# Four large PSUM tiles in place of three large and two small ones, from the seventh token group of the up phase on

## The chip, the cores and the metric

The kernel runs on one core of a Trainium2 chip. The metric is the time on the device in microseconds (us); a kernel's time is the median of its runs.

## The reference

```python
x = _attn_ref(q, k, v, tau)            # 2304 tokens x 512
x = _moe_ref(x, modality_id, ...)      # one of 8 experts per token
logits = x @ w_gate
P = np.exp(logits - logits.max())
for _ in range(8):
    P /= P.sum(1, keepdims=True) + 1e-09
    P /= P.sum(0, keepdims=True) + 1e-09
    P *= N / E
for e in range(E):                     # 8 experts, all of them for every token
    h = np.maximum(x @ w1[e], 0.0)     # 512 -> 1024
    out += P[:, e:e + 1] * (h @ w2[e]) # 1024 -> 512
```

The change touches the last loop, the dense mixture, in which every token goes through all 8 experts.

## The kernel before, in words

The program has three stretches: attention, the routed mixture, and the dense mixture. The dense mixture has an *up phase* (`x @ w1`, `up()`, L1142) and a *down phase* (`h @ w2`, the loop at L1422). Both use Strassen's scheme: a matrix product in 2 x 2 blocks is made of seven block products, numbered 0 to 6, whose sums give the four output blocks. float32 is kept by splitting each operand into a rounded part and a rest, and by adding three products of these; the two parts are made by `both()` (L939): ScalarE casts (L937), VectorE subtracts (L941).

Up phase: 8 experts, two column halves of each, three token groups: `n_up` = 48 groups, counted by `n` (L1329). In each group `product()` (L1129) issues 12 matmuls of 128 x 384 for each of the seven block products, in the order `ORD` = 0, 2, 1, 4, 3, 6, 5 (L90). After each product VectorE and ScalarE read the finished PSUM tile (L1172 to L1200), and `hook(b)` then issues pieces of other work.

Three large PSUM tiles A, B, C of two banks each take the products. In a group they have three roles: `ch` takes products 0, 1, 3 and 5, one added to the other; `cc` takes product 2; `cb` takes product 4 and then, from a fresh start, product 6. The roles move on by one tile from group to group (L1144).

Who reads them, on ScalarE's and VectorE's queues:

- after 0, 1 and 3, ScalarE copies `ch` to x (L1173, L1175, L1181);
- after 1, VectorE adds `cc` into h12; after 3, it adds `cc` into h22 and weighs h22 (L944, L1137);
- after 4, VectorE adds `cb` into h11 and weighs h11;
- after 6, VectorE adds `cb` into h12, weighs it, and forms two differences on VectorE and one on GpSimd;
- after 5, VectorE weighs `ch` into h21 and forms one more difference.

"Weigh" is `weigh()` (L1136): the larger of the value and 0, times the token's weight. All seven results are stored to DRAM (`save()`, L1152).

The weights of the next column half are made in every third group (`u == 2`, L1347): `make_up()` (L964) puts one cast on ScalarE and one subtraction on VectorE (L941, `w1c<-wr` or `w1c<-x`) behind each product, and GpSimd makes two of their sums.

Two small PSUM tiles of one bank each (`small()`, L987) serve the gate in the first six groups, by the generators `steps` and `later`. They stay open to the end of the up phase. Then they are closed, and a fourth large tile D takes their place (L1366, L1367). The down phase uses all four: each token group holds one tile over four experts, and `buf()` (L1370) hands them out in turn.

The order on each engine's queue is that in which the program calls the instructions (`manual_schedule`, L1478).

Of the kernel before, what the change touches and what calls it, by code (L numbers as in the profile page):

```python
# [7 lines left out]
F32 = mybir.dt.float32  # L8
# [7 lines left out]
PSUM = bass.MemoryType.PSUM  # L16
DRAM = bass.MemoryType.DRAM

B, H, S, D = 4, 8, 576, 64
# [69 lines left out]
UN = 384  # L89
# [8 lines left out]
def _program(ctx, tc, qT, kT, vv, tau, wg, mod, mbias, cst, wA, wg2, wU, wD, out):  # L98
    nc = tc.nc
    P = 128  # L100
# [8 lines left out]
    pd = dram.tile([2, 72, P], F32, name="pd")  # L109
# [665 lines left out]
    def experts(es):  # L775
# [167 lines left out]
        def op2(eng, out, x, y, op):  # L943
            eng.tensor_tensor(out=out, in0=x, in1=y, op=op)  # L944

        def cut(t, lo, k, n):
            return t[:, lo:lo + k * n].rearrange("p (k n) -> p k n", k=k)
# [35 lines left out]
        ps_m = es.enter_context(tc.tile_pool(name="pm", bufs=1, space=PSUM, reuse_waits="tile"))  # L983
        pt_s = ExitStack()
        ps_t = pt_s.enter_context(tc.tile_pool(name="pt2", bufs=2, space=PSUM, reuse_waits="tile"))
        bank = lambda tag: ps_m.tile([P, 2, 512], F32, tag=tag, name="q" + tag)
        small = lambda: ps_t.tile([P, 512], F32, tag="t", name="t")  # L987

        X = [[[cut(t, (2 * b + i) * 2 * UN, 2, UN) for i in range(2)] for b in range(7)] for t in (xb, xa, xc)]
# [134 lines left out]
        def load_p(dst, e, u):  # L1124
            for t in range(2):
                nc.sync.dma_start(
                    out=dst[t], in_=pd[t].rearrange("(e u t) n -> e u (t n)", e=E, u=NU)[e, u].partition_broadcast(P))

        def product(q, first, a, b, nk):  # L1129
            for j, (l, r) in enumerate(((0, 0), (1, 0), (0, 1))):  # L1130
                for i in range(2):
                    for k in range(nk):
                        mm(q[:, i, 0:UN], lhsT=a[l][:, k, 128 * i:128 * i + 128], rhs=b[r][:, k],  # L1133
                           start=first and k == 0 and j == 0, stop=k == nk - 1 and j == 2, skip_group_check=True)

        def weigh(out, src, pv, n=2):  # L1136
            V.scalar_tensor_tensor(out=out, in0=src, scalar=0.0, in1=bc(pv.unsqueeze(1), [P, n, UN]), op0=ALU.max, op1=ALU.mult)  # L1137

        def relu(out, src):
            A.activation(out=out, in_=src, func=AF.Relu)  # L1140

        def up(n, e, g, u, hook):  # L1142
            order = (0, 4, 2, 1, 6, 3, 5) if n < 3 else ORD
            ch, cb, cc = (bank("ABC"[(i - n) % 3])[:, :, 0:UN] for i in range(3))  # L1144
            where = {0: ch, 1: ch, 3: ch, 5: ch, 2: cc, 4: cb, 6: cb}
            h11, h12, h22, h21 = quad[n if n < 3 else n % 2]
            if n == 0:
                h11 = cut(pbx, 720, 2, UN)
            t1, t2, t3, t4 = quad[2]
            pv = pbs[n % 2]  # L1150

            def save(b, src):  # L1152
                nc.sync.dma_start(out=hd[e, u, b, :, 2 * g:2 * g + 2], in_=src)

            todo = []

            def fin(x, src, t, b):
                if e:
                    weigh(x, src, pv[t])
                    save(b, x)  # L1160
                elif src is x:
                    todo.append((x, b))
                else:
                    relu(x, src)
                    save(b, x)

            plus = lambda out, x, y: op2(V, out, x, y, ALU.add)
            minus = lambda eng, out, x, y: op2(eng, out, x, y, ALU.subtract)
            for b in order:
                product(where[b], b in (0, 2, 4, 6), wu[b], X[u][b], 2)  # L1170
                ready, todo[:] = list(todo), []
                if b == 0:  # L1172
                    A.copy(out=h11, in_=ch)  # L1173
                elif b == 1:
                    A.copy(out=h12, in_=ch)  # L1175
                    plus(h12, cc, h12)
                elif b == 4:
                    plus(h11, cb, h11)
                    fin(h11, h11, 0, 0)
                elif b == 3:  # L1180
                    A.copy(out=h22, in_=ch)  # L1181
                    plus(h22, cc, h22)
                    fin(h22, h22, 1, 6)
                elif b == 6:
                    plus(h12, cb, h12)
                    if e:
                        weigh(h12, h12, pv[1])
                        minus(V, t1, h12, h11)
                        save(2, t1)
                        minus(G, t3, h22, h12)  # L1190
                        minus(V, t2, h22, t1)
                        save(1, t2)
                        save(3, t3)
                    else:
                        fin(h12, h12, 1, 2)
                elif b == 5:
                    fin(h21, ch, 0, 4)
                    if e:
                        minus(V, t4, h21, t2)
                        save(5, t4)  # L1200
                for x, s in ready:
                    relu(x, x)
                    save(s, x)
                hook(b)
# [8 lines left out]
        def chained(*its):  # L1213
            for it in its:
                yield from it
# [21 lines left out]
        xs, steps, later = chained(xs, make_x(1), make_x(2)), gates(), sink()  # L1237
        D = {}
# [90 lines left out]
        for n in range(n_up):  # L1329
            k, u = divmod(n, NU)  # L1330
            e, g = divmod(k, 2)

            def hook(b):
                at = (ORD if n >= 3 else (0, 4, 2, 1, 6, 3, 5)).index(b)
                for _ in range(2):
                    next(xs, None)
                if next(steps, False) is False and (n > 2 or n == 2 and at > 2):
                    next(later, None)
                if 2 * NU - 1 <= n < n_up - 1 and at == (1 if n >= 2 * NU else 5):
                    e2, u2 = divmod(n + 1, 2 * NU)  # L1340
                    load_p(pbs[(n + 1) % 2], e2, u2 % NU)
                if k < 2 * E - 1:
                    if (u, at) == ((0, 0) if k else (1, 2)):
                        ld_up(k + 1)
                    elif u == 1 and at in (4, 6):
                        sums_up(k + 1, at // 2 - 2)
                    elif u == 2:  # L1347
                        make_up(k + 1, b)
                elif u == 1:
                    if at == 0:  # L1350
                        w_load(0, 0, 0)
                        h_load(0)
                        for j in range(1, 4):
                            w_load(0, j, 0)
                    elif at == 6:
                        w_make(0)
                elif u == 2:
                    if at in (0, 3, 6):
                        h_make(at // 3)

            up(n, e, g, u, hook)
            if n == n_up - NU:
                open_down()

        open_rest()
        pt_s.close()  # L1366
        ps_d = es.enter_context(tc.tile_pool(name="pd", bufs=1, space=PSUM, reuse_waits="tile"))  # L1367
        turns = [0]

        def buf(tag=None):  # L1370
            if tag is None:
                tag = "ABCD"[turns[0] % 4]
                turns[0] += 1
            return (ps_d if tag == "D" else ps_m).tile([P, 2, 512], F32, tag=tag, name="r" + tag)

        done, half, sent = [0], [None], []

        def put(*tiles):
            q = buf("CCCCDCADC"[done[0]])
            done[0] += 1  # L1380
            at = [9 * t + 3 * u + j for u, t, j in tiles]
            for h, i in enumerate(at):
                for d in range(4):
                    nc.tensor.transpose(q[:, h, 128 * d:128 * d + 128], x2[:, d, 128 * i:128 * i + 128], ident)
            o = D["o"][done[0] % 4]
            A.copy(out=o, in_=q)
            for h, i in enumerate(at):
                G.memset(idx_0, 0)
                ins = G.indirect_dma_start(out=out, in_=o[:, h], in_offset=None,
                                           out_offset=bass.IndirectOffsetOnAxis(ap=idx_c[:, i:i + 1], axis=0))  # L1390
                for x in sent:
                    tc.declare_no_dep(ins.ins if hasattr(ins, "ins") else ins, x, reason="rows of a permutation")
                sent.append(ins.ins if hasattr(ins, "ins") else ins)
# [27 lines left out]
        q = [None] * NU  # L1421
        for n, (m, u) in enumerate(SEQ):  # L1422
            i, b, e = STEPS[m]
# [54 lines left out]
    with tc.manual_schedule():  # L1478
        with ExitStack() as es:
            attention(es)  # L1480
        with ExitStack() as es:
            experts(es)
# [88 lines left out]
```

## Time and profile before

| | us |
|---|---|
| runs of the kernel | 2083.52, 2086.37, 2086.32 |
| median | 2086.32 |
| the profiled execution, its own time | 2085.2 |
| its span, first to last instruction | 2083.4 |
| TensorE busy in it (PE) | 2000.8 |
| VectorE busy (DVE) | 1560.4 |
| ScalarE busy (ACT) | 870.8 |
| GpSimd busy (POOL) | 484.6 |

All times in the trace are counted from the start of the span. The up phase runs from about 583.6 to 1320.8 us, the down phase from there to the end. The trace gives start and duration of each instruction, and for idle time what ended it. A matmul's row is its own time of 0.33 us; in a row of matmuls they overlap, so a product of 12 matmuls has a duration of 2.24 us while the next product starts 2.08 us after it. Starts, not durations, tell how fast TensorE advances. Names are the program's: qA is large tile A in the up phase, rA the same in the down phase.

### The profile page before, as it was taken

The numbers are of one execution on the slowest core, as the hardware profiler recorded it, in microseconds if no ns is written. First come the engines' busy times: TensorE is split into PE (matmuls) and PEld (weight loads), VectorE is DVE, ScalarE is ACT, GpSimd is POOL, SyncE is SP. The second block draws the span as 40 slices with busy tenths as digits, with TensorE's granted clock in tenths as the row PEclk, the third lists the DMA queues.
The fourth block names the chain that finished last, engine by engine and source line by source line (L and its number), as shares of the span: only waits on it lengthen the run. The fifth ranks groups of instructions, "written<-read, shape, count | busy, mean of one in ns | idle before, by whom it ended". The sixth has DMA issues, their size and how long they took to land.

```text
span 2083.4 us, 32556 instructions
## 1 busy us (share of the span) xinstructions
PE 2000.8 (96%) x12677; PEld 1906.7 (92%) x12677; DVE 1560.4 (75%) x1957; ACT 870.8 (42%) x1152; POOL 484.6 (23%) x395
## 2 busy tenths in 40 slices
PE   8999998999989999999999999999999999899997
PEld 7777777999979999999999999999999999899997
DVE  7788886666576799888989898856766568777672
ACT  6777763555554322222222222444443443343433
POOL 5564625052021233232333232000000000000004
PEclk9999998999999999999999999999999999999999
DMA  5232324666523566766676776965565776776753
GB/s 191 74 120 98 98 64 155 203 204 207 187 84 107 195 224 226 244 239 233 226 238 219 240 244 219 405 243 182 185 213 203 247 270 244 254 264 242 252 209 131
DMA packets 177215, 421.12 MB, mean 202 GB/s; under 512 B 16397, under 2 KB 126365, under 8 KB 177053
## 3 DMA queue, kind: packets, MB, share of 16 engines
q1 hardware_dynamic: 170700, 399.03, 56.1%
q0 software_dynamic: 4928, 19.93, 2.5%
q8 instruction: 102, 1.67, 0.3%
q14 instruction: 61, 0.49, 0.1%
q10 hardware_dynamic: 1424, 0.01, 0.0%
HBM read 274.91 MB, written 143.99 MB: 201 GB/s over the span
## 4 chain that ended last, share of the span: by engine, by line
PE 38%; DVE 13%; issue 12%; DMA 5%; ACT 2%; POOL 0%; SPq 0%; POOLq 0%; ACTq 0%; DVEq 0%
PE rB L1431 6%; PE rA L1431 6%; PE rD L1431 6%; PE qB L1133 5%; PE rC L1431 5%; PE qC L1133 5%; PE qA L1133 5%; DVE x L944 5%; DVE x L1137 3%; DMA pbx<-pd 3%; DVE w1c L941 2%; DVE df L944 1%; DVE xa L941 1%; ACT xa L937 1%; DMA hd<-x 1%
## 5 line engine op out<-in xcount | busy, mean ns | idle before, releaser
L944 POOL TENSOR_TENSOR x<-x 128x768 f32<-128x768 f32 x45 | 114.9, 2554 | 462.2 <-DVE x L1137 368.3
L941 DVE TENSOR_TENSOR w1c<-df,w1c 128x1536 fp32r<-128x1536 f32 x84 | 146.4, 1756 | 88.5 <-ACT w1c L937 88.4
L941 DVE TENSOR_TENSOR xa<-df,xa 128x1536 fp32r<-128x1536 f32 (+1 forms) x100 | 166.6, 1670 | 59.7 <-ACT xa L937 59.5
L937 ACT CAST xa<-df 128x1536 fp32r<-128x1536 f32 (+1 forms) x100 | 140.4, 1412 | 157.5 <-DVE df L944 69.3
L944 DVE TENSOR_TENSOR x<-x 128x768 f32<-128x768 f32 x135 | 196.3, 1454 | 4.9 <-DVE xb L944 0.5
L937 ACT CAST w1c<-df 128x1536 fp32r<-128x1536 f32 x84 | 123.5, 1481 | 147.0 <-DVE df L944 55.9
L1324 POOL DMA_DIRECT2D hd<-df x12 | 6.6, 550 | 612.4 <-DVE df L944 612.4
L1133 PE MATMUL qB<-xc,w1c 128*128 128x384 f32 x768 | 143.7, 335 | 2.9 <-DVE x L944 1.9
L1133 PE MATMUL qC<-xa,w1c 128*128 128x384 f32 x768 | 144.0, 335 | 1.5 <-ACT x L1181 1.5
L1133 PE MATMUL qA<-xb,w1c 128*128 128x384 f32 x768 | 144.0, 335 | 0.2 <-ACT x L1181 0.2
L478 DVE TENSOR_REDUCE cols<-s 128x1 f32<-128x576 f32 x144 | 105.0, 755 | 51.7 <-PE s L473 51.0
L1133 PEld LDWEIGHTS qB<-xc,w1c 128*128 128x128 f32 x768 | 133.9, 188 | 3.5 <-issue 2.2
L1133 PEld LDWEIGHTS qA<-xb,w1c 128*128 128x128 f32 x768 | 134.0, 188 | 2.7 <-issue 2.1
L1133 PEld LDWEIGHTS qC<-xa,w1c 128*128 128x128 f32 x768 | 133.7, 188 | 1.8 <-ACT x L1181 1.8
L489 ACT ACTIVATE sa<-s,cols 128x576 f32<-128x576 f32 x144 | 103.4, 741 | 65.2 <-DVE cols L478 65.2
L1137 DVE SCALAR_TENSOR_TENSOR x<-x,pbx 128x768 f32<-128x768 f32 x126 | 125.8, 999 | 4.3
L172 DVE TENSOR_TENSOR colr<-cols,colr 128x1024 fp32r<-128x1024 f32 x57 | 72.8, 1281 | 56.4 <-ACT colr L171 56.2
L473 PE MATMUL s<-colr 128*128 128x288 f32 x640 | 110.0, 310 | 4.6 <-DVE cols L500 1.2
L1431 PE MATMUL rA<-xa 128*128 128x384 f32 x576 | 105.9, 339 | 5.7 <-ACT xa L937 5.7
L1431 PEld LDWEIGHTS rA<-xa 128*128 128x128 f32 x576 | 101.4, 190 | 6.6 <-ACT xa L937 6.6
L473 PEld LDWEIGHTS s<-colr 128*128 128x128 f32 x640 | 89.1, 189 | 18.8 <-issue 14.3
L1431 PE MATMUL rB<-w1c,xa 128*128 128x384 f32 x552 | 99.8, 335 | 0.0
(292 smaller groups left out, 4451.7 us busy)
## 6 DMA issues: line engine op xcount, KB each, us to landing
df<-hd SPq DMA_DIRECT2D x180, 768.0 KB, 4.9
hd<-x SPq DMA_DIRECT2D x317, 384.0 KB, 3.1
cols<-wA SPq DMA_DIRECT2D x84, 512.0 KB, 4.6
pbx<-pd SPq DMA_DIRECT2D x114, 192.0 KB, 5.1
wr<-wU SPq DMA_DIRECT2D x16, 768.0 KB, 6.2
dg<-wD SPq DMA_DIRECT2D x20, 512.0 KB, 8.0
hd<-df POOLq DMA_DIRECT2D x12, 768.0 KB, 7.3
cols<-qT SPq DMA_DIRECT2D x15, 576.0 KB, 4.1
```

What stands on the lines that cost most here:

```text
L172: sub.tensor_tensor(out=lo[i], in0=raw, in1=hi[i].bitcast(F32), op=ALU.subtract)
L473: mm(s[:, hf, 0:288], lhsT=l, rhs=r, start=n == 0, stop=n == len(ops) - 1)
L478: V.tensor_reduce(out=mx[:, i % 18:i % 18 + 1], in_=St[i][:, :, 0:288], axis=AX.XY, op=ALU.max, negate=True)
L489: A.activation(out=e.rearrange("p (h c) -> p h c", h=2), in_=St[i][:, :, 0:288], func=AF.Exp, bias=mxs[i // 18 % 2][0][:, i % 18:i % 18 + 1])
L937: A.copy(out=out, in_=in_)
L941: sub.tensor_tensor(out=hi_lo[1], in0=src, in1=hi_lo[0].bitcast(F32), op=ALU.subtract)
L944: eng.tensor_tensor(out=out, in0=x, in1=y, op=op)
L1133: mm(q[:, i, 0:UN], lhsT=a[l][:, k, 128 * i:128 * i + 128], rhs=b[r][:, k], start=first and k == 0 and j == 0, stop=k == nk - 1 and j == 2 ...
L1137: V.scalar_tensor_tensor(out=out, in0=src, scalar=0.0, in1=bc(pv.unsqueeze(1), [P, n, UN]), op0=ALU.max, op1=ALU.mult)
L1324: G.dma_start(out=hd[0, u, b], in_=x)
L1431: mm(q[u][:, i2, 0:UN], lhsT=a[l][:, k, 128 * i2:128 * i2 + 128], rhs=h[r][:, k], start=first and k == 0 and j == 0, stop=last and k == 3 ...
```

## The change

From group `n` = 6 on (`NOLD`), the two small tiles are closed and tile D is open in their place. The gate's generator is run to its end first; after the sixth group it has nothing left to issue. Each group then has four roles: `ch` for products 0, 1, 3 and 5, `cb` for product 4, `cd` for product 6, and `cc` for product 2. `cc` is D in every group; A, B and C rotate: a group's `ch` is the group before's `cb`, its `cb` that group's `cd`, and its `cd` that group's `ch`. The down phase hands out the same four tiles, beginning with the last group's `cb`, then `cc`, `cd` and `ch`, and its output steps take the same turns under the new names.

```diff
+        NOLD, role, ps_4 = 6, [], []
+        bank = lambda tag: (ps_4[0] if tag == "D" else ps_m).tile([P, 2, 512], F32, tag=tag, name="q" + tag)
...
         def up(n, e, g, u, hook):
-            ch, cb, cc = (bank("ABC"[(i - n) % 3])[:, :, 0:UN] for i in range(3))
-            where = {0: ch, 1: ch, 3: ch, 5: ch, 2: cc, 4: cb, 6: cb}
+            if n < NOLD:
+                ch, cb, cc = (bank("ABC"[(i - n) % 3])[:, :, 0:UN] for i in range(3))
+                cd = cb
+            else:
+                if n == NOLD:
+                    role[:] = ["ABC"[(2 - n + 1) % 3], "ABC"[(1 - n + 1) % 3], "D", "ABC"[(1 - n) % 3]]
+                else:
+                    role[:] = [role[1], role[3], role[2], role[0]]
+                ch, cb, cc, cd = (bank(r)[:, :, 0:UN] for r in role)
+            where = {0: ch, 1: ch, 3: ch, 5: ch, 2: cc, 4: cb, 6: cd}
...
-                    plus(h12, cb, h12)
+                    plus(h12, cd, h12)
...
+            if n == NOLD:
+                for _ in later:
+                    pass
+                pt_s.close()
+                ps_4.append(es.enter_context(tc.tile_pool(name="pd", bufs=1, space=PSUM, reuse_waits="tile")))
             up(n, e, g, u, hook)
...
-        pt_s.close()
-        ps_d = es.enter_context(tc.tile_pool(name="pd", bufs=1, space=PSUM, reuse_waits="tile"))
+        spare = "".join(role[i] for i in (1, 2, 3, 0))
...
-                tag = "ABCD"[turns[0] % 4]
+                tag = spare[turns[0] % 4]
...
-            q = buf("CCCCDCADC"[done[0]])
+            q = buf(spare[(2, 2, 2, 2, 3, 2, 0, 3, 2)[done[0]]])
```

The number and order of the instructions stay the same on every engine; the tiles that they name change, and with these the waits. TensorE's queue, before, in one group in which weights are made (n = 26, operand `xc`, seven products in the order 0, 2, 1, 4, 3, 6, 5) and the first four products of the next (n = 27, operand `xb`):

```order
L1133 MATMUL qB<-xc,w1c 128x384 x12
L1133 MATMUL qA<-xc,w1c 128x384 x12
L1133 MATMUL qB<-xc,w1c 128x384 x12
L1133 MATMUL qC<-xc,w1c 128x384 x12
L1133 MATMUL qB<-xc,w1c 128x384 x12
L1133 MATMUL qC<-xc,w1c 128x384 x12
L1133 MATMUL qB<-xc,w1c 128x384 x12
L1133 MATMUL qA<-xb,w1c 128x384 x12
L1133 MATMUL qC<-xb,w1c 128x384 x12
L1133 MATMUL qA<-xb,w1c 128x384 x12
L1133 MATMUL qB<-xb,w1c 128x384 x12
```

The same eleven products on TensorE's queue with the change:

```order
L1134 MATMUL qB<-xc,w1c 128x384 x12
L1134 MATMUL qD<-xc,w1c 128x384 x12
L1134 MATMUL qB<-xc,w1c 128x384 x12
L1134 MATMUL qA<-xc,w1c 128x384 x12
L1134 MATMUL qB<-xc,w1c 128x384 x12
L1134 MATMUL qC<-xc,w1c 128x384 x12
L1134 MATMUL qB<-xc,w1c 128x384 x12
L1134 MATMUL qA<-xb,w1c 128x384 x12
L1134 MATMUL qD<-xb,w1c 128x384 x12
L1134 MATMUL qA<-xb,w1c 128x384 x12
L1134 MATMUL qC<-xb,w1c 128x384 x12
```

Product 6 (sixth row) no longer follows product 4 (fourth row) into the same tile, and the next group's product 4 (last row) no longer goes into the tile that held product 5 (seventh row), but into product 6's.

TensorE's queue at the end of the up phase, before: the last two products of the last group (6 and 5) and the first four steps of the down phase:

```order
L1133 MATMUL qC<-xc,w1c 128x384 x12
L1133 MATMUL qB<-xc,w1c 128x384 x12
L1431 MATMUL rA<-xa 128x384 x24
L1431 MATMUL rB<-xa 128x384 x24
L1431 MATMUL rC<-w1c,xa 128x384 x24
L1431 MATMUL rA<-w1c,xa 128x384 x24
```

The same place on TensorE's queue with the change:

```order
L1134 MATMUL qC<-xc,w1c 128x384 x12
L1134 MATMUL qB<-xc,w1c 128x384 x12
L1444 MATMUL rA<-xa 128x384 x24
L1444 MATMUL rD<-xa 128x384 x24
L1444 MATMUL rC<-w1c,xa 128x384 x24
L1444 MATMUL rA<-w1c,xa 128x384 x24
```

The down phase's second step moves from B, the tile of product 5, to D, which in the last group held product 2.

## Rows read from the trace of the kernel before

**Rows 1.** The page: busy time, share of the span and instructions of TensorE.

```profile
PE 2000.8 (96%) x12677; PEld 1906.7 (92%) x12677; DVE 1560.4 (75%) x1957; ACT 870.8 (42%) x1152; POOL 484.6 (23%) x395
```

**Rows 2.** Stretch, length, busy PE, PEld, DVE, ACT, POOL, clock, DMA share, GB/s.

```profile
690.11:1320.84 630.73, 619.28 (x3529) 610.64 (x3529) 556.41 (x552) 162.05 (x225) 194.83 (x93) 1.00 0.70 237
```

**Rows 3.** Waits of TensorE, 690 to 1322 us: total us, times, longest us.

```profile
PE qB L1133 <- DVE x L1137: 8.0, 13, 0.6
PE qC L1133 <- DVE x L944: 3.3, 13, 0.3
```

**Rows 4.** Timeline of TensorE, groups 26 to 29: start, us, instruction, [idle before].

```profile
998.29 2.25 PE L1133 MATMUL qB<-xc,w1c 128*128 128x384 f32 x12
1000.80 2.35 PE L1133 MATMUL qC<-xc,w1c 128*128 128x384 f32 x12 [0.26 <-DVE x L944]
1002.99 2.24 PE L1133 MATMUL qB<-xc,w1c 128*128 128x384 f32 x12
...
1009.23 2.25 PE L1133 MATMUL qA<-xb,w1c 128*128 128x384 f32 x12
1012.09 2.38 PE L1133 MATMUL qB<-xb,w1c 128*128 128x384 f32 x12 [0.62 <-DVE x L1137]
1014.31 2.24 PE L1133 MATMUL qA<-xb,w1c 128*128 128x384 f32 x12
...
1035.11 2.24 PE L1133 MATMUL qB<-xc,w1c 128*128 128x384 f32 x12
```

**Rows 5.** Timeline of VectorE in the same stretch.

```profile
994.09 0.94 DVE L1137 SCALAR_TENSOR_TENSOR x<-qC,pbx 128x768 f32<-128x768 f32 x1
...
999.18 0.69 DVE L941 TENSOR_TENSOR w1c<-wr,w1c 128x512 fp32r<-128x512 f32 x1 [0.96 <-ACT w1c L937]
999.79 0.95 DVE L944 TENSOR_TENSOR x<-qC,x 128x768 f32<-128x768 f32 x1
...
1002.25 0.95 DVE L944 TENSOR_TENSOR x<-qA,x 128x768 f32<-128x768 f32 x1
...
1005.12 0.94 DVE L944 TENSOR_TENSOR x<-qC,x 128x768 f32<-128x768 f32 x1
...
1011.09 0.94 DVE L1137 SCALAR_TENSOR_TENSOR x<-qB,pbx 128x768 f32<-128x768 f32 x1
...
1014.51 0.96 DVE L944 TENSOR_TENSOR x<-qB,x 128x768 f32<-128x768 f32 x1
...
1017.42 0.96 DVE L944 TENSOR_TENSOR x<-qC,x 128x768 f32<-128x768 f32 x1 [0.96 <-ACT x L1181]
...
1027.87 0.96 DVE L944 TENSOR_TENSOR x<-qB,x 128x768 f32<-128x768 f32 x1 [1.16 <-ACT x L1175]
```

**Rows 6.** Busy time summed over the three groups from 989.98 to 1035.11 us.

```profile
sum 45.13, PE 44.25 PEld 43.61 DVE 40.22 ACT 11.25 POOL 14.59; mean PE 14.75 PEld 14.54 DVE 13.41 ACT 3.75 POOL 4.86
```

**Rows 7.** Timeline, all engines, end of the up phase: TensorE and VectorE.

```profile
1319.08 0.95 DVE L944 TENSOR_TENSOR x<-qA,x 128x768 f32<-128x768 f32 x1
...
1320.84 4.33 PE L1431 MATMUL rA<-xa 128*128 128x384 f32 x24
...
1326.29 0.94 DVE L1137 SCALAR_TENSOR_TENSOR x<-qB,pbx 128x768 f32<-128x768 f32 x1
...
1327.29 4.46 PE L1431 MATMUL rB<-xa 128*128 128x384 f32 x24 [2.12 <-DVE x L1137]
...
1331.48 4.56 DVE L941 TENSOR_TENSOR xa<-df,xa 128x1536 fp32r<-128x1536 f32 x3
1331.59 4.32 PE L1431 MATMUL rC<-w1c,xa 128*128 128x384 f32 x24
...
1342.68 1.22 DVE L941 TENSOR_TENSOR xa<-df,xa 128x1024 fp32r<-128x1024 f32 x1
```

**Rows 8.** The main DMA queue, 1280 to 1345 us: packets, MB, share.

```profile
q1 hardware_dynamic: 10062, 22.63, 91.5%
```

**Rows 9.** Timeline of TensorE, down phase, at its longest early wait.

```profile
1376.16 6.03 PE L1431 MATMUL rD<-xa 128*128 128x384 f32 x24 [2.81 <-ACT xa L937]
```

More of the change, by code (lines that the diff above doesn't have):

```diff
@@ L985, in experts @@
         ps_t = pt_s.enter_context(tc.tile_pool(name="pt2", bufs=2, space=PSUM, reuse_waits="tile"))
-        bank = lambda tag: ps_m.tile([P, 2, 512], F32, tag=tag, name="q" + tag)
+        NOLD, role, ps_4 = 6, [], []
+        bank = lambda tag: (ps_4[0] if tag == "D" else ps_m).tile([P, 2, 512], F32, tag=tag, name="q" + tag)
         small = lambda: ps_t.tile([P, 512], F32, tag="t", name="t")
@@ L1371, in buf @@
             if tag is None:
-                tag = "ABCD"[turns[0] % 4]
+                tag = spare[turns[0] % 4]
                 turns[0] += 1
-            return (ps_d if tag == "D" else ps_m).tile([P, 2, 512], F32, tag=tag, name="r" + tag)
+            return (ps_4[0] if tag == "D" else ps_m).tile([P, 2, 512], F32, tag=tag, name="r" + tag)
         done, half, sent = [0], [None], []
         def put(*tiles):
-            q = buf("CCCCDCADC"[done[0]])
+            q = buf(spare[(2, 2, 2, 2, 3, 2, 0, 3, 2)[done[0]]])
             done[0] += 1
```

## The prediction

> **What bounds the kernel now.** I read the page first: TensorE is busy 2000.8 of 2083.4 us [rows 1], so only what makes it wait, or what it does more slowly, can move the end. [...] These are 42 groups of seven products, 294 products. Where nothing waits, a product starts 2.08 us after the one before: from 1014.31 to 1035.11 us, ten products take 20.80 us [rows 4]. 294 x 2.08 is 611.5 us. So 630.7 - 611.5 = **19.2 us** of the stretch are lost to waits.
>
> The table of waits says where: TensorE waits for VectorE at two places only, 13 times each, once for a weigh (L1137) and once for an addition (L944) [rows 3]. The timeline of one period of three groups shows both. The reader is to compare starts with 2.08 us:
>
> - In group 26, product 6 starts at 1000.80, 2.51 us after product 3 (0.43 too much), and the next starts 2.19 us later (0.11 too much, the load of weights having waited as well) [rows 4]. It waits since it goes into C, which holds product 4 until VectorE has added it to h11: 999.79 + 0.95 = 1000.74 [rows 5].
> - In group 27, product 4 starts at 1012.09, 2.86 us after product 1 (0.78), and the next 2.22 us later (0.14) [rows 4]. It goes into B, which holds group 26's product 5 until the weigh at 1011.09 ends at 1012.03 [rows 5].
>
> Together 1.46 us. The period of three groups tells the same: 45.13 us [rows 6] against 21 x 2.08 = 43.68, 1.45 us lost. VectorE is late there since group 26 is one in which weights are made: seven more subtractions stand in its queue, and at 999.18 it stood still for 0.96 us for a cast [rows 5], with the addition that frees C behind.
>
> **The change, part by part.** *No work is added or removed.* The queues hold the same instructions in the same order; only tiles and waits differ. Running out the gate's generator issues nothing, and D needs the two small tiles to be read, which happened before group 6: 0 us, since no queue is passed.
>
> *Does each product find its tile free?* I take VectorE's times of group 26 as they are (its queue is full through the group, and what it waits for there is ScalarE's cast, not TensorE), and let TensorE go every 2.08 us from product 3 at 998.29. Then product 6 starts at 1000.37, product 5 at 1002.45, and in group 27 products 0, 2, 1, 4, 3, 6, 5 at 1004.53, 1006.61, 1008.69, 1010.77, 1012.85, 1014.93, 1017.01. Against these stand the last reads of the new tiles [rows 5]:
>
> - product 6 of group 26 needs the tile of group 25's product 5, weighed by 994.09 + 0.94 = 995.03: 5.3 us to spare;
> - product 0 of group 27 needs product 4's, read by 1000.74: 3.8 us;
> - product 2 needs D, read by 1002.25 + 0.95 = 1003.20: 3.4 us;
> - product 4 needs product 6's, read by 1005.12 + 0.94 = 1006.06: 4.7 us;
> - product 6 needs product 5's, read by 1012.03: 2.9 us, the smallest;
> - product 0 of group 28 (1019.09) needs product 4's of group 27, read by 1014.51 + 0.96 = 1015.47: 3.6 us.
>
> So neither wait is followed by another, and the 1.45 us go from the period, **if VectorE keeps up**. It is busy 40.22 of 45.13 us [rows 6]; the new period has 43.68, so 3.5 us of idle time stay. And it must catch up before the next group with weights. It does so at once: at 1017.42 it had waited 0.96 us for ScalarE's copy of product 3, which now comes 1.45 us sooner, so it starts at 1016.46 and is 0.5 us behind; at 1027.87 it had waited 1.16 us for the copy of product 1, and 0.66 us of that are left [rows 5]. From there on everything is 1.45 us earlier, VectorE too. The wait that is left is again VectorE's for TensorE, not the reverse.
>
> Thirteen periods give 13 x 1.45 = 18.9 us, and the last group's product 6, whose wait of the same kind is followed by no group, the rest of the 19.2 us. I take 19.2. Bounds: nothing, if VectorE were the limit; 19.2, since no more is lost there.
>
> *The start of the down phase.* The second step starts at 1327.29, 6.45 us after the first, where 24 matmuls take 4.16 (two products); the third starts 4.30 us after it. Lost are 2.29 + 0.14 = 2.4 us [rows 7]. It waits for the weigh of product 5 (1326.29 to 1327.23), since it goes into that tile. Now it goes into D, read by 1319.08 + 0.95 = 1320.03, and can start right after the first. What is late next? The fourth step's weights: three subtractions run from 1331.48 to 1336.04 behind the group's rest on VectorE [rows 7], whose end does not move; the one for weights is the second; it lasts 1.22 us like the one at 1342.68, which leaves about 1.7 for each of the others, so it is done at about 1334.4 [rows 7]. The fourth step would start at 1333.0 and use it a third of the way in, at 1334.4. That just fits; I allow 0.1 us. The transfers are near their limit there, 91.5% of 16 engines [rows 8], which could hold back a step; below, this costs the whole 2.4, above, nothing. I take 2.3, as the steps' operands lie loaded four ahead.
>
> *Later.* The waits of the down phase follow TensorE's own products through ScalarE and VectorE (the longest early one, 2.81 us, ends with a cast [rows 9]), so they move with it: 0 us. This is not free of risk: after that wait, 24 matmuls took 6.03 instead of 4.32 us, so 1.7 us hang on how long a wait lasts. I allow 4 us either way.
>
> Sum: 19.2 + 2.3 = **21.5 us**. The profiled execution took 2085.2 us, so 2063.7; it stands 1.1 us below the median of the runs, 2086.3. From the median: **2064.8 us**.
>
> **The rivals.** A measurement of this kernel can tell about 0.2%, 4.2 us, from no change.
>
> *A. VectorE carries its lateness on.* For: it is busy 89% of the period, and part of its idle time is forced, such as the 0.96 us at 999.18. If it did not recover by group 29, its lateness would add up until product 6 or 2 waits: the margins are 2.9 and 3.4 us. Against: the two waits worked out above absorb 1.45 us with 0.66 to spare. If half the gain went back, 9.6 + 2.3 = 11.9 us: 2074.4. Chance 0.07.
>
> *B. VectorE sets the period.* Then it stays 45.13 us, the waits only move to other products, and just the 2.3 us of the down phase's start remain: 2084.0, no change. Against: 40.22 us busy. Chance 0.04. [...]
>
> *C. The start of the down phase gives nothing,* as the transfers hold it: 19.2 us, 2067.1. Chance 0.10.
>
> *D. The clock falls: slower.* Group 26 writes four tiles in turn instead of three. [...] For: the 6.03 us after a long wait [rows 9]. Against: with 26 waits of up to 0.6 us the clock stood at 1.00 throughout [rows 2, 3]. Chance 0.02. [...]
>
> **How the numbers follow.** The forecast, both parts gained, has 0.77; with C, 0.87 lie between 2060 and 2069. The range also takes in A and, below, 4 us of the down phase and 2 of spread between runs (2083.5 to 2086.4): 2058 to 2075. Outside are B, D and mishaps. Faster by over 0.2%: the forecast, A and C, 0.94. Within 0.2%: B, 0.04. Slower: D, 0.02.
>
> **What would show it.** Right: the table of waits has no row of TensorE for VectorE from group 6 on; 294 products take 611.5 us; VectorE's busy time stays, at 91 to 92% of a period of 43.68 us; its waits for ScalarE's copies shrink; the down phase's second step starts 4.16 us after the first. Wrong: a new wait at product 6 or 2 (A, B); a clock below 1.00 in the up phase (D); an equal up phase with a longer wait for casts in the down phase (C).

## The result, and the profile after

The changed kernel takes 2064.3 us (median of 4 runs, 2060.44 to 2067.65) against 2086.35 us (4 runs, 2083.52 to 2087.44): a ratio of 0.9897, 95% interval 0.9883 to 0.9911. In a second set of runs it took 2066.0 us against 2085.87 us, 0.9905 (0.989 to 0.9921). The forecast was 2064.8 us.

Busy time of the stretch from group 6's first product to the down phase's first step, in the columns of [rows 2]:

```profile
694.13:1305.65 611.52, 611.52 (x3529) 611.52 (x3529) 553.63 (x552) 162.34 (x225) 194.84 (x93) 1.00 0.72 244
```

630.73 us [rows 2] have become 611.52, and TensorE is busy in all of them. VectorE does the same work (553.63 us; 556.41 before). The table of waits has no row of TensorE left from 690 to 1300 us, where [rows 3] had two. Its timeline in groups 26 to 29, to be held against [rows 4]:

```profile
993.65 2.24 PE L1134 MATMUL qB<-xc,w1c 128*128 128x384 f32 x12
995.73 2.24 PE L1134 MATMUL qC<-xc,w1c 128*128 128x384 f32 x12
997.81 2.24 PE L1134 MATMUL qB<-xc,w1c 128*128 128x384 f32 x12
...
1004.05 2.24 PE L1134 MATMUL qA<-xb,w1c 128*128 128x384 f32 x12
1006.13 2.24 PE L1134 MATMUL qC<-xb,w1c 128*128 128x384 f32 x12
...
1010.29 2.24 PE L1134 MATMUL qB<-xb,w1c 128*128 128x384 f32 x12
```

Product 6 of group 26 (995.73) and product 4 of group 27 (1006.13) start 2.08 us after their forerunners, and so do all others: ten of them lie between 985.33 and 1006.13 us. VectorE in the same stretch, to be held against [rows 5], and the sum over the three groups, against [rows 6]:

```profile
995.15 0.95 DVE L944 TENSOR_TENSOR x<-qA,x 128x768 f32<-128x768 f32 x1
...
1006.45 0.94 DVE L1138 SCALAR_TENSOR_TENSOR x<-qB,pbx 128x768 f32<-128x768 f32 x1
...
1011.63 0.95 DVE L944 TENSOR_TENSOR x<-qD,x 128x768 f32<-128x768 f32 x1
...
1021.78 0.96 DVE L944 TENSOR_TENSOR x<-qD,x 128x768 f32<-128x768 f32 x1 [0.86 <-ACT x L1184]
```

```profile
sum 43.68, PE 43.68 PEld 43.68 DVE 40.03 ACT 11.27 POOL 14.59; mean PE 14.56 PEld 14.56 DVE 13.34 ACT 3.76 POOL 4.86
```

VectorE is as late in group 26 as before: its addition for product 4 still runs at 995.15, 9.82 us after the group's first product (985.33; before, 999.79 - 989.98 = 9.81). Nobody waits for it any more. The wait of 0.96 us for the copy of product 3 is gone (1011.63 has none), that of 1.16 us for the copy of product 1 has shrunk to 0.86.

The start of the down phase, timeline of TensorE (PE, and PEld, its weight loads), against [rows 7]:

```profile
1305.65 4.32 PE L1444 MATMUL rA<-xa 128*128 128x384 f32 x24
...
1309.81 4.32 PE L1444 MATMUL rD<-xa 128*128 128x384 f32 x24
...
1313.97 4.32 PE L1444 MATMUL rC<-w1c,xa 128*128 128x384 f32 x24
...
1318.13 4.55 PE L1444 MATMUL rA<-w1c,xa 128*128 128x384 f32 x24
...
1319.63 2.74 PEld L1444 LDWEIGHTS rA<-w1c,xa 128*128 128x128 f32 x16 [0.27 <-DVE xa L941]
```

The second and third step start 4.16 us after their forerunners, where it was 6.45 and 4.30 [rows 7]. The fourth waits a little for its weights (0.27 us of idle weight loads) and loses 0.24 us: the fifth step starts at 1322.53, 4.40 us after it.

The profiled execution of the changed kernel, the slowest of its four runs, took 2067.65 us, 17.6 less than that of before, though the two terms alone give 19.2 + 2.3. The other 4 us lie ahead of group 6, which starts at 694.13 us instead of 690.11. No edit lies there. From 583 to 690 us the granted clock was 0.95 in this profile and 0.98 in that of before; in the nine experiments' profiles group 6 starts between 691.3 and 694.6.

### The profile page after: what moved, and what is told of

The parts are those of the page before. It is cut to its first block, busy times and chain, and to the rows that moved or that the text cites. A ratio compares the mean times of both kernels' runs of the same rounds, so it can differ in the third digit from the quotient of the medians.

```text
span 2065.9 us, 32516 instructions
## 1 busy us (share of the span) xinstructions
PE 1998.4 (97%) x12677; PEld 1910.6 (92%) x12677; DVE 1557.4 (75%) x1957; ACT 871.9 (42%) x1152; POOL 486.0 (24%) x395
## 3 DMA queue, kind: packets, MB, share of 16 engines
q8 instruction: 102, 1.67, 0.3%
## 4 chain that ended last, share of the span: by engine, by line
PE 58%; DVE 7%; ACT 2%; issue 2%; DMA 0%; POOL 0%; POOLq 0%; ACTq 0%; DVEq 0%; SPq 0%
PE qB L1134 10%; PE qC L1134 9%; PE qA L1134 9%; PE rB L1444 7%; PE rD L1444 7%; PE rA L1444 6%; PE rC L1444 6%; PE qD L1134 4%; DVE df L944 2%; DVE xa L941 2%; ACT xa L937 1%; DVE x L944 1%; DVE w1c L941 1%; ACT w1c L937 1%; DVE dg L944 1%
## 5 line engine op out<-in xcount | busy, mean ns | idle before, releaser
L944 DVE TENSOR_TENSOR x<-qD,x 128x768 f32<-128x768 f32 x84 | 80.0, 953 | 31.2 <-ACT x L1184 16.8
```

## Experiments

**1. Product 6 alone gets a tile.**

```diff
-                if n == NOLD:
-                    role[:] = ["ABC"[(2 - n + 1) % 3], "ABC"[(1 - n + 1) % 3], "D", "ABC"[(1 - n) % 3]]
-                else:
-                    role[:] = [role[1], role[3], role[2], role[0]]
+                role[:] = ["ABC"[(i - n) % 3] for i in range(3)] + ["D"]
...
-        spare = "".join(role[i] for i in (1, 2, 3, 0))
+        spare = "".join(role[i] for i in (2, 0, 1, 3))
```

> Edit: only product 6 gets a tile of its own (D); A, B and C keep the old roles and rotation, and the down phase keeps its old order of tiles. Theory (both waits of a period are one and the same lateness of VectorE, and the last one decides): product 6 no longer waits, but product 4 of the next group still needs the tile of product 5, which VectorE gives back at the same time as before, so its wait grows by the 0.54 us saved, from 0.78 to about 1.3 us; the period stays at 45.13 us and the time at 2086 us (2083 to 2088). Rival (the waits add up, each is worth its own length): 14 x 0.54 = 7.5 us gained, 2079 us.

Measured: 2087.56 us against 2087.46, ratio 1.000 (0.9991 to 1.001). The table of waits of TensorE, 690 to 1322 us, and its timeline around the two old places:

```profile
PE qB L1134 <- DVE x L1138: 14.9, 13, 1.1
```

```profile
999.93 2.24 PE L1134 MATMUL qB<-xc,w1c 128*128 128x384 f32 x12
1002.01 2.24 PE L1134 MATMUL qD<-xc,w1c 128*128 128x384 f32 x12
...
1010.33 2.24 PE L1134 MATMUL qA<-xb,w1c 128*128 128x384 f32 x12
1013.72 2.35 PE L1134 MATMUL qB<-xb,w1c 128*128 128x384 f32 x12 [1.15 <-DVE x L1138]
```

Product 6 (1002.01) no longer waits; product 4 of the next group starts 3.39 us after product 1, 1.31 too much where it had been 0.78. The period stays at 45.10 us. Both waits are one lateness, and the last to end decides: a tile for product 6 alone is worth nothing. (The 42 groups took 630.20 us, 0.5 less than before. The down phase's first two steps took 2.15 us more: the second waited 2.71 us instead of 2.12, and its matmuls were slower.)

**2. Product 4 alone leaves product 5's tile.**

```diff
-                if n == NOLD:
-                    role[:] = ["ABC"[(2 - n + 1) % 3], "ABC"[(1 - n + 1) % 3], "D", "ABC"[(1 - n) % 3]]
-                else:
-                    role[:] = [role[1], role[3], role[2], role[0]]
+                role[:] = ["ABC"[-n % 3], "D", "ABC"[(2 - n) % 3], "D"]
...
-        spare = "".join(role[i] for i in (1, 2, 3, 0))
+        spare = role[2] + role[0] + "D" + "ABC"[(1 - n_up + 1) % 3]
```

> Edit: products 4 and 6 share D, one after the other as before; products 0, 1, 3, 5 and product 2 rotate over A, B, C, so that no product 4 follows a product 5 into its tile; the down phase's second step still goes into the last product 5's tile. Theory: the wait of product 4 goes (13 x 0.92 us), that of product 6 stays (0.43 + 0.11 us in 14 groups): 12 us gained, 2074 us (2072 to 2077); the table of waits has one row, product 6 for an addition, 13 or 14 times 0.26. Rival (what is saved behind comes back in front, at product 6): VectorE would be later for product 6 by what TensorE gains, the wait of 0.43 grows towards 1.3 us and the time stays at 2086 us.

Measured: 2076.32 us against 2087.46, ratio 0.9953 (0.9936 to 0.9969). The table of waits, and the timeline at product 6 of group 26:

```profile
PE qD L1134 <- DVE x L944: 3.4, 13, 0.3
```

```profile
994.43 2.24 PE L1134 MATMUL qB<-xc,w1c 128*128 128x384 f32 x12
996.94 2.37 PE L1134 MATMUL qD<-xc,w1c 128*128 128x384 f32 x12 [0.27 <-DVE x L944]
999.15 2.24 PE L1134 MATMUL qB<-xc,w1c 128*128 128x384 f32 x12
```

Product 4's wait is gone, product 6's is unchanged (2.51 and 2.21 us between starts). The period is 44.28 us, 0.85 below 45.13. 11.1 us gained where 12 were expected. Together with run 1: the change needs both moves for the whole, but only the second is worth anything alone.

**3. The down phase's second step back in product 5's tile.**

```diff
-        spare = "".join(role[i] for i in (1, 2, 3, 0))
+        spare = "".join(role[i] for i in (1, 0, 3, 2))
```

> Edit: the changed kernel, with the down phase's second step in the tile of the last product 5, as before the change. Theory: the up phase keeps its gain, the second step starts 6.5 to 6.9 us after the first instead of 4.16, and nothing later takes this back: 2.3 to 2.7 us more than the changed kernel, about 2067 us. Rival (the start of the down phase is held by transfers or casts anyway): the step after waits less or a later wait shrinks, and the down phase ends as early as in the changed kernel, 2064 us.

Measured: 2070.01 us against 2087.46, ratio 0.9918 (0.9902 to 0.9935), so 2.7 to 4.4 us above the changed kernel by its two ratios; the intervals overlap, so these times alone don't settle it. TensorE's timeline, and the stretch of the second step in the columns of [rows 2]:

```profile
1302.79 4.32 PE L1444 MATMUL rA<-xa 128*128 128x384 f32 x24
1309.65 6.03 PE L1444 MATMUL rB<-xa 128*128 128x384 f32 x24 [2.53 <-DVE x L1138]
1315.52 4.32 PE L1444 MATMUL rC<-w1c,xa 128*128 128x384 f32 x24
```

```profile
1309.65:1315.52 5.87, 5.87 (x25) 5.87 (x26) 5.87 (x5) 3.63 (x3) 0.00 (x0) 0.71 1.04 393
```

The wait costs 2.70 us (6.86 - 4.16), as expected. Not expected: the step behind it takes 5.87 instead of 4.16 us, at a granted clock of 0.71, against 1.00 in the step before and the step after. So in this execution the missing D cost 4.4 us at the first steps, though the same wait, 0.4 us shorter, had cost only 2.4 before. The 1.7 us of the slower step are not its fixed price; the last section shows that the same wait is not always followed by a slow step. The whole down phase took 7.5 us more than in the changed kernel's first profile: among other things, two later waits for casts grew from 2.79 to 4.81 us and from 4.18 to 5.07. The edit changes the order of the tiles there too; why these waits grew was not tried.

**4. More lateness in the kernel before.** In `make_up()`:

```diff
             both(wu[b], (a11, a11, sas[k > 0], a21, a12, a22s[k > 0], a12)[b], cp, sub)
+            if sub is V and b in (0, 2, 1):
+                sub.tensor_tensor(out=wu[b][1], in0=(a11, a11, sas[k > 0], a21, a12, a22s[k > 0], a12)[b], in1=wu[b][0].bitcast(F32), op=ALU.subtract)
```

> Edit: the kernel before, with VectorE's subtraction for the weights of products 0, 2 and 1 issued twice (the same values written again): 3 x 0.65 = 1.95 us more of VectorE per period, of which the wait of 0.96 us for a cast hides about 0.7. Theory (TensorE waits for VectorE's lateness in the group with weights): each period grows by 1.2 to 1.95 us, 13 times: 16 to 25 us slower, 2102 to 2111 us, with both waits longer. Rival (the waits come from somewhere else, such as the tiles' rotation alone): the idle time of VectorE, 4.9 us in a period, takes the work in, 2086 us.

Measured: 2125.09 us against 2087.46, ratio 1.0188 (1.0171 to 1.0205): 37.6 us slower, where 16 to 25 were expected. In its profile the 42 groups took 663.70 us, 33.0 more than before. Timelines of TensorE and VectorE in group 26, and the group's row by stretch:

```profile
1016.87 2.24 PE L1135 MATMUL qB<-xc,w1c 128*128 128x384 f32 x12
1021.46 3.85 PE L1135 MATMUL qC<-xc,w1c 128*128 128x384 f32 x12 [2.35 <-DVE x L944]
1025.15 2.24 PE L1135 MATMUL qB<-xc,w1c 128*128 128x384 f32 x12
```

```profile
1016.68 1.66 DVE L967 TENSOR_TENSOR w1c<-x,w1c 128x512 fp32r<-128x512 f32 x1
...
1020.45 0.95 DVE L944 TENSOR_TENSOR x<-qC,x 128x768 f32<-128x768 f32 x1
```

```profile
1008.55:1027.23 18.68, 16.33 (x86) 16.01 (x86) 18.37 (x20) 5.85 (x9) 7.40 (x4) 0.91 0.53 186
```

The addition that frees C runs 11.90 us after the group's start instead of 9.81: 2.09 us later, more than the 1.2 to 1.95 expected, as the second repeated subtraction took 1.66 us. Product 6's wait grows by as much (4.59 us between starts, 2.51 too much). Again the clock adds to it, 0.91 in the group's row: the product behind the wait takes 3.69 us, 1.61 too much. The 0.92 us at product 4 are swallowed. 2.09 + 1.50 - 0.92 = 2.67: from the fifth period on, 47.8 instead of 45.13 us. (After the first three waits, as long as the others, the next product starts after 2.21 or 2.22 us, not 3.69. These periods take 46.33, 47.19 and 47.19 us.) So VectorE's lateness does reach TensorE, against the rival; the size was missed by the longer subtraction and by the clock.

**5. The same lateness in the changed kernel,** with the same edit.

> Edit: the changed kernel, with VectorE's subtraction for the weights of products 0, 2 and 1 issued twice: 1.95 us more of VectorE per period, 42.2 of 43.68 us. Theory: VectorE is 1.2 to 1.95 us later in the group with weights, less than the smallest margin of 2.9 us, and catches up in the next two groups; no wait of TensorE, 2064 us (2060 to 2068). Rival A (VectorE carries lateness on): waits at products 6 or 2 from the second or third period on, up to 13 x 1.95 us = 25 us, 2075 to 2090 us.

Measured: 2068.87 us against 2086.64, ratio 0.991 (0.989 to 0.9931). Busy time, 690 to 1300 us, VectorE's weigh of group 26's product 5, and the sum over the three groups from 984.61:

```profile
690.00:1300.00 610.00, 610.00 (x3521) 610.00 (x3520) 587.33 (x589) 158.25 (x226) 195.52 (x94) 1.00 0.71 241
```

```profile
1007.80 0.95 DVE L1140 SCALAR_TENSOR_TENSOR x<-qB,pbx 128x768 f32<-128x768 f32 x1
```

```profile
sum 43.68, PE 43.68 PEld 43.68 DVE 42.80 ACT 11.07 POOL 14.56; mean PE 14.56 PEld 14.56 DVE 14.27 ACT 3.69 POOL 4.85
```

TensorE does not wait once in this stretch. The weigh ends at 1008.75, and product 6 of group 27 starts at 984.61 + 12 x 2.08 = 1009.57: 0.8 us of the margin of 2.9 are left, 2.1 used. VectorE is at 42.80 of 43.68 us. The time itself lies 0.9 us above the expected range of 2060 to 2068; run 9 shows where the repeats still cost something.

**6. Lateness beyond the margins:** the changed kernel with the subtraction repeated behind all seven products (the condition is `sub is V`).

> Edit: the changed kernel, with VectorE's subtraction for the weights issued twice behind all seven products: 7 x 0.65 = 4.5 us more of VectorE per period, 44.7 us of work against 43.68. Theory (fourth tile gives cover, VectorE's work per period is the next limit): the period becomes VectorE's, 44.7 to 45.7 us, so 1.0 to 2.0 us x 13 = 13 to 26 us slower than the changed kernel, 2077 to 2090 us, with VectorE at 98% or more of the up phase. Rival (TensorE stalls as soon as a margin is used up, whatever VectorE's sum): each period grows by the whole 4.5 us, 58 us, 2122 us.

Measured: 2105.97 us against 2086.64, ratio 1.0086 (1.0069 to 1.0103), some 40 us above the changed kernel, where the theory had 13 to 26 and the rival 58. Waits of TensorE from 690 to 1350 us, and one period of three groups:

```profile
PE qB L1136 <- DVE x L1140: 17.0, 13, 1.3
PE qD L1136 <- DVE x L944: 4.9, 12, 0.4
```

```profile
sum 46.37, PE 44.58 PEld 43.62 DVE 45.51 ACT 10.96 POOL 14.54; mean PE 14.86 PEld 14.54 DVE 15.17 ACT 3.65 POOL 4.85
```

VectorE is at 45.51 of 46.37 us, 98%, and sets the period, as the theory had it. The size was off: the seven repeats cost 5.5 us, not 4.5, so the period is 46.35 us and the up phase 33.6 us longer (645.11 - 611.52). The down phase is 6.9 us longer as well, which the theory did not have. The waits stand where the margins were smallest: at product 6, which needs product 5's tile (2.9 us), and at product 2, which needs D (3.4 us).

**7. The weights of the down phase one token group earlier.** The edit is in the loop at L1422:

```diff
             if m < NM - 3:
-                if u == 1:
+                if u == 0:
                     w_make(m + 1)
```

> Edit: the changed kernel, with the down phase's weights for the next step made one token group earlier (behind the first instead of the second of three). Theory (the waits of the down phase follow TensorE's own products through a cast that stands late in ScalarE's queue): the waits at a change of block product (1.1 to 4.4 us, some ten of them, about 25 us in all) become shorter, 5 to 20 us gained, 2045 to 2060 us. Rival (merging the results on VectorE or the transfers set these waits): they stay or move, 2064 us or some us more.

Measured: 2042.55 us against 2086.64, ratio 0.9788 (0.9771 to 0.9804). TensorE's longest waits in the down phase of the changed kernel, and then in this one:

```profile
PE rB L1444 <- ACT xa L937: 10.1, 4, 3.7
PE rC L1444 <- ACT xa L937: 8.5, 3, 4.2
PE rA L1444 <- ACT xa L937: 6.6, 4, 4.0
```

```profile
PE rB L1444 <- ACT xa L937: 3.2, 1, 3.2
PE rA L1444 <- ACT w1c L937: 2.4, 1, 2.4
PE rC L1444 <- ACT xa L937: 2.1, 1, 2.1
```

The down phase, from its first matmul to the start of its last, shrinks from 749.32 to 724.87 us. At the first change of block product, the changed kernel's ScalarE and TensorE, and then this kernel's:

```profile
1357.68 1.04 ACT L937 CAST xa<-dg 128x1024 fp32r<-128x1024 f32 x1 [2.96 <-DVE dg L944]
...
1358.78 7.17 PE L1444 MATMUL rB<-xa 128*128 128x384 f32 x24 [2.81 <-ACT xa L937]
```

```profile
1352.03 1.05 ACT L937 CAST xa<-dg 128x1024 fp32r<-128x1024 f32 x1 [2.96 <-DVE dg L944]
...
1354.31 4.32 PE L1444 MATMUL rB<-xa 128*128 128x384 f32 x24
```

The cast now ends 1.2 us before the step that needs it, and the slow matmuls behind the wait (7.17 us for 24) are gone with it. The gain is larger than the 5 to 20 us expected, and this version beats both kernels, the changed one by 22 us.

**8 and 9. The changed kernel and run 5's kernel once more, on one chip.** No edit, and the edit of run 5.

> No edit: the changed kernel once more, beside the next run on one chip. Theory: 0.9897 of the kernel before, up phase from group 6 on 611.5 us and down phase's first three steps 4.16 us apart; what moves between its runs lies before group 6 and in the waits of the down phase. Rival (part of the gain in the first result was the spread of few runs): a ratio nearer to 1, such as 0.993.

> Edit: the changed kernel with the subtraction issued twice behind products 0, 2 and 1, once more, on the same chip as the run above. Theory (VectorE's 2.1 us more per period are covered in all 13 periods; only the group before the down phase has nothing to cover it): the up phase's 42 groups take 611.5 us, the down phase's first steps lose 0.5 to 2 us, the time is 0.5 to 2 us above the run above. Rival (they cost a little everywhere): 3 us or more above it, with waits in the up phase.

Measured: the changed kernel 2066.0 us, ratio 0.9905 (0.989 to 0.9921); with the repeated subtractions 2069.36 us, 0.992 (0.9906 to 0.9934), both against 2085.87. The up phase's 42 groups take 611.52 us in both profiles. In run 8 group 6 starts 1.7 us earlier than in the first profile of the changed kernel, and the down phase takes 0.7 us more. With the repeats the first steps of the down phase wait twice for VectorE:

```profile
PE rA L1446 <- DVE xa L941: 1.4, 1, 1.4
PE rC L1446 <- DVE w1c L941: 0.4, 1, 0.4
```

That is 1.8 us; the medians are 3.4 us apart, with overlapping intervals. The theory had 0.5 to 2, the rival 3 or more. But the rival's waits from group 6 on do not exist. In the profiles the rest lies ahead of group 6, which starts at 692.43 in run 8 and at 694.58 in run 9. Product 6 of group 5, the last group on the three old tiles, in run 8 and in run 9:

```profile
688.16 2.35 PE L1134 MATMUL qC<-xc,w1c 128*128 128x384 f32 x12
```

```profile
690.31 2.35 PE L1136 MATMUL qC<-xc,w1c 128*128 128x384 f32 x12 [1.53 <-DVE x L944]
```

It starts 0.13 us after the matmuls in front of it in run 8, 1.91 us in run 9, as it waits for VectorE's addition of product 4, the old wait. Run 5's profile has the same wait of 1.53 us (at 689.12). So the repeats cost 1.8 us where the fourth tile is not yet open, and up to 1.8 us where the up phase ends; between them they cost nothing. In the kernel before, the same repeats cost 37.6 us.

## Why the prediction was right, step by step

- *19.2 us lost to two waits per period*: the stretch went from 630.73 us [rows 2] to 611.52, 19.21. Every period is 43.68 us, as worked out.
- *No new wait follows, smallest margin 2.9 us*: in the changed kernel the weigh of product 5 ends at 1007.39 and product 6 of group 27 starts at 1010.29, 2.90 us later. Runs 5 and 6 show that the margin is real: 2.1 us of lateness pass unseen in the up phase, more come back as waits at the two places that rival A named.
- *VectorE catches up by group 29*: the wait for the copy of product 3 went, that for the copy of product 1 was forecast at 0.66 and is 0.86 us.
- *2.3 us at the start of the down phase*: it came to 2.2. The 2.43 us of the second and third step are gone, and the fourth, for which 0.1 us was allowed, lost 0.24. In run 3's one profile, without D as second tile, 4.4 us were lost there.
- *0 us in the later down phase, 4 either way*: the sum held, its reason did not. The whole down phase took 2.34 us less (751.66 to 749.32), so 0.15 us is left for the later part. But the waits there did not move along unchanged. Three of them went from 4.74, 3.52 and 0.46 us to 2.79, 4.18 and 1.89, and in run 8 they are 2.77, 4.05 and 1.89, so this comes with the change. The steps behind waits also took longer or shorter by up to 1.4 us, and not according to how long the wait lasts, on which the prediction let 1.7 us hang: behind the same wait of 2.81 us, 24 matmuls took 5.87 us before and 7.01 after, at granted clocks of 0.71 and 0.58. That all this adds up to 0.15 us is luck; in run 8 the down phase took 0.7 us more.
- *Rival B* (VectorE sets the period) became true only with 5.5 us more work per period, run 6. *Rival C* (transfers hold the down phase's start) did not come: the steps followed each other at 4.16 us. *Rival D* (the clock) did not come: it stood at 1.00 through the stretch, with four tiles in turn. But no idle time was left there. Run 6 had some: four tiles in turn with 25 waits of up to 1.3 us, and a clock of 1.00 over its 645.11 us. The clock did fall in runs 3 and 4, after waits of 2.53 and 2.35 us, to 0.71 over the next step and 0.91 over the group.

One thing the prediction treated loosely: it counted the two waits as 0.54 + 0.92 us. Their sum is right, but they don't add up as parts. Run 1 shows the first to be worth nothing alone.

That the median, 2064.3 us, lies 0.5 us from the forecast is in part luck: the four runs spread from 2060.44 to 2067.65, and in the second set the gain was 19.9 us where 21.5 were forecast.

## What to carry to other kernels

When an engine waits twice in a period for the same late partner, removing the first wait can just move it to the second, as in run 1, where 0.78 us became 1.31; list every tile's last read against the start of its next write, and change the rotation so that all margins exceed the lateness. Here the smallest margin, worked out from one timeline as 2.9 us, measured 2.90, and the 42 groups took 611.52 us where 611.5 were forecast. The margins also tell how much more work the partner can take before the waits return: in run 5, 2.1 us more lateness against a margin of 2.9 brought none. Run 6 shows the other limit: with the partner busy for 98% of the period, the waits are back although the fourth tile is there. That a further buffer would not help then is argued, not tried.

## What the runs showed of the hardware that was not expected

A wait of TensorE can have a second price: the matmuls behind it may run at a lower granted clock. After 2.53 us of idle time (run 3) the next 24 took 5.87 instead of 4.16 us, at a granted clock of 0.71; after 2.35 us (run 4) the next 12 took 3.69 instead of 2.08 us, at 0.91 over the group. [rows 9] had shown such a case: after 2.81 us, 5.87 us at 0.71. In the changed kernel's first profile the clock was 0.50 from 1358.78 to 1364.00 us, right behind its wait of 2.81 us. What was not expected is that the length of the wait alone does not decide. The same step of the same kernel, in its first profile and in run 8:

```profile
1413.47 4.43 PE L1444 MATMUL rC<-xa 128*128 128x384 f32 x24 [1.76 <-ACT xa L937]
```

```profile
1410.31 6.02 PE L1444 MATMUL rC<-xa 128*128 128x384 f32 x24 [1.76 <-ACT xa L937]
```

After the same 1.76 us the next step starts 4.27 us later in the one and 5.86 in the other, at granted clocks of 1.00 and 0.71. The wait of 2.81 us at the first change of block product stands in ten of the eleven profiles (2.80 in run 1); behind it 24 matmuls took anything from 4.29 us (run 9) to 7.01 (the changed kernel's first profile). In run 4 the product behind each of the first three waits of 2.35 us took 2.21 or 2.22 us, behind the ten later ones it was slower. So what such a wait costs beyond its own length can't be read from one profile. What decides was not tried.

A VectorE subtraction that lasts 0.69 us elsewhere took 1.66 us when it was repeated in run 4. It started at 1016.68, while GpSimd's sum ran, from 1016.21 to 1017.79 us. The other rows of this subtraction, 700 to 1290 us in runs 4, 5 and 6, point the same way. The 12, 13 and 13 that took 1.66 or 1.67 us all started while such a sum was running; those that started some 0.25 us ahead of one took 0.68 or 0.69, and none of the rest took over 0.69. That the sum is the cause is likely by this, but no run without it was made.
